# Top-k attention with a low-rank mixer on one core: side work of the vector engine handed to the scalar and pool engines

## The chip, the core and the metric

The kernel runs on one NeuronCore of a Trainium2 chip. Five engines take part, each with its own in-order queue of instructions. TensorE (PE, with its weight loads shown apart as PEld) does the matmuls and transposes. VectorE (DVE) does the search for the largest scores. ScalarE (ACT) does exponentials and copies out of PSUM. GpSimd (POOL) does elementwise work in SBUF. SyncE (SP) issues most transfers. The metric is the device time of one execution in microseconds (us). A result is the median over runs.

## What is computed

The attention keeps, for every query, only the 32 largest of 576 scores. Its output, with the heads laid side by side, is the input `x` of a mixer: a rank-32 map over the sequence is added to it (`u`), and a two-layer MLP over the channels is added to that.

```python
# q, k, v: (8, 8, 576, 64) fp32; U (576, 32), V (32, 576), w_ch1 (512, 2048), w_ch2 (2048, 512): fp64
scores = scale * q @ k.T
kth = the 32nd largest of each row
scores = where(scores >= kth, scores, -1e9)
attn = exp(scores - max); attn = attn / (attn.sum() + 1e-9)
x = (attn @ v), heads side by side          # (8, 576, 512)
u = x + (x.T @ U @ V).T
out = u + relu(u @ w_ch1) @ w_ch2
```

q, k and v are fp32. U, V and the two weight matrices arrive as 64-bit floats, and the kernel turns them into 32-bit floats by integer arithmetic on their words.

## The kernel before

**Pairs, tiles and steps.** The 64 heads are taken as 32 pairs `g`, four pairs to a batch. The 576 rows of a pair are five tiles `t`: tiles 0 to 3 have 128 rows and hold two score chunks of 128 x 576 (one for each head); tile 4 (`t == NT`) has the 64 last rows of both heads stacked into one chunk. One tile is one step `n`, so a pair has five steps and the run 160.

**One step.** `scores` does the matmuls, and ACT copies the scores to SBUF (lines 288 to 290; line 280 for tile 4). `front` then runs the search on DVE, for every chunk: MAX8 (line 315), then three times MATCH_REPLACE8 and MAX8 (lines 327 and 331). The 32nd value is the threshold. Chunk 0 is weighed early: ACT takes the exponential (line 295), and after the search one DVE operation zeroes what is under the threshold and sums the row (the mask, line 335). Chunk 1 goes the other way: after the search POOL adds -3e38 to scores under the threshold in two operations (lines 333 and 334), and ACT takes the exponential and the sum afterwards. Tile 4 has only chunk 0, so it is masked on DVE. `turns` transposes the weights on PE (line 363, and line 368 for the tails), with ACT copying them out; `values` multiplies by v (lines 383, 393 and 396).

**The mixer.** When a pair's five tiles are done, `mixed` transposes its output on PE (line 417), one DVE operation multiplies it by the reciprocals of the row sums into `x` (line 419), and some slots later PE multiplies by U (line 430) and V (line 442), giving `uT`. When a batch's four pairs are there, `mlp` starts: matmuls with w_ch1 (line 467), relu on ACT (line 479), matmuls with w_ch2 (line 486), one DVE operation that adds `uT` and writes `oT` (line 499), and `turned_back`, which transposes `oT` on PE (line 511) and stores it. `turned_back` is put off by a few matmuls (lines 480 and 493).

**The order.** PE and ACT run in exactly the order in which the program is written. DVE and POOL are ordered by a scheduler that goes by readiness in its own model of time, with `high_priority` blocks (lines 379, 418 and 498) put first when ready. The MLP of a batch is a generator; `fill` takes a measured share of it in eight slots of every step of the next batch, so that PE alternates between attention and MLP. The first 21 steps (`n <= ALONE`, batch 0) have no MLP to fill in. The MLP of batch 7 comes after the last step.

**The parameters.** 36 pieces of 64-bit parameters (four small ones for U and V, 32 of 128 x 512 for the weights) go through three buffers `raw`. One call of `next_params` joins the piece before (`f64_join`), splits the piece that has landed (`f64_parts`) and issues the next transfer on SP. Splitting is an Abs and an Identity on ACT (lines 152 and 154) and a maximum on POOL (line 153). Joining is a shift-and-mask on DVE (line 160), an and-or of the exponent's top bits from the high word on DVE (line 168) and an integer add on POOL of the low part (line 172), which is the last reader of `raw`. On DVE the join is ordered behind the last mask. One piece is taken in each step of batch 0, two in each step from step 21 until all are done.

Of the kernel before, what the change touches and what calls it, by code (L numbers as in the profile page):

```python
# [8 lines left out]
F32 = mybir.dt.float32  # L9
# [12 lines left out]
def kernel(  # L22
# [82 lines left out]
    half_bit = const.tile([P, 1], F32, name="half_bit")  # L105
    nc.vector.memset(half_bit, 1.0 / 64)
# [30 lines left out]
    def f64_parts(raw, out):  # L137


        n, w = raw.shape[0], raw.shape[-1] // 2  # L140
# [13 lines left out]
        nc.scalar.activation(low, low8, AF.Identity, bias=half_bit[0:n], scale=1.0 / 32)  # L154
        return hi, bits, low

    def f64_join(hi, bits, low, outs):


        ins = nc.vector.tensor_scalar(  # L160
            bits, bits, 3, 0x3FFFFFFF, ALU.logical_shift_left, ALU.bitwise_and
        )
        if last_mask:
# [4 lines left out]
        nc.vector.scalar_tensor_tensor(  # L168
            out=bits, in0=hi, scalar=0xC0000000, in1=bits, op0=ALU.bitwise_and, op1=ALU.bitwise_or
        )  # L170
# [47 lines left out]
    def load(g):  # L218
# [3 lines left out]
        for name, src in (("q", q), ("k", k)):  # L222
            queue = nc.scalar if g == 0 and name == "k" else nc.sync
            t = loads.tile([P, NT, 2, D], F32, tag=f"ld_{name}", name=f"ld_{name}")
            for i in range(2):
                queue.dma_start(
                    t[:, :, i, :],
                    src[b, h0 + i, 0:MAIN, :].rearrange("(p t) d -> p t d", t=NT),
                )
            queue.dma_start(  # L230
# [12 lines left out]
    def prep(g):  # L243
# [4 lines left out]
        for i, t in enumerate(tiles):  # L248
# [3 lines left out]
            nc.scalar.copy(qkT[:, i, 0:MAIN], tp.rearrange("p t n -> p (t n)"))  # L252
# [8 lines left out]
    def scores(g, t):  # L261
# [26 lines left out]
        nc.scalar.copy(main[:, :, 0:HALF], scs[0][:, :, 0:HALF])  # L288
# [8 lines left out]
    def front(g, t):  # L297
# [10 lines left out]
        probs[g, t] = E2  # L308
        curs, ms = list(chunks), [None] * n
# [13 lines left out]
        weigh(chunks[0], Es[0], nmax[:, 0:1])  # L323
        for i in range(1, TOPK // 8):
# [4 lines left out]
            for c in order:  # L329
                ms[c] = small.tile([P, 8], F32, tag="m8", name="m8", bufs=8)  # L330
                nc.vector.max(ms[c], curs[c])  # L331
        if n == 2:
            nc.gpsimd.tensor_scalar(Es[1], chunks[1], ms[1][:, 7:8], NEG, ALU.is_lt, ALU.mult)  # L333
            nc.gpsimd.tensor_tensor(chunks[1], chunks[1], Es[1], ALU.add)  # L334
        ins = nc.vector.scalar_tensor_tensor(  # L335
            out=Es[0],
            in0=chunks[0],
            scalar=ms[0][:, 7:8],
            in1=Es[0],
            op0=ALU.is_ge,  # L340
            op1=ALU.mult,
            accum_out=sums[0],
        )
# [4 lines left out]
        if n == 2:  # L348
            weigh(chunks[1], Es[1], nmax[:, 1:2], sums[1])
# [58 lines left out]
    def mixed(g, wait):  # L408
# [9 lines left out]
        with tc.high_priority():  # L418
            nc.vector.tensor_tensor(
# [37 lines left out]
    def mlp(b):  # L457
# [3 lines left out]
        for chunks, (lo, hi) in zip(PARTS, SPAN):  # L461
            w = hi - lo
            hTs = []
            for f in range(NF):
# [15 lines left out]
                if f == 1 and late:  # L480
                    late.pop()()
# [171 lines left out]
```

## Time and profile before

| | us |
|---|---|
| three runs | 1920.41, 1916.99, 1920.29 |
| median | 1920.29 |
| the profiled execution | 1917.73 |
| its span, first to last instruction | 1915.9 |

| engine | busy us | share of the span | instructions |
|---|---|---|---|
| PE | 1772.1 | 92% | 10528 |
| PEld | 1335.0 | 70% | 10528 |
| DVE | 1654.0 | 86% | 3433 |
| ACT | 953.4 | 50% | 2345 |
| POOL | 571.8 | 30% | 346 |

Busy time is the union of an engine's instructions. Idle time costs something only on the engine that sets the pace of a stage, and here this is not the same engine in all stages. The order of the masks on DVE gives a clock for the steps: the mask of step 0 starts at 22.38 us, that of step 20 at 247.65, of step 28 at 358.87, of step 40 at 485.40 and that of the last step, 159, at 1760.27.

### The profile page before, as it was taken

To read this page: it belongs to the slowest core of one execution; us is meant where nothing else is said; L and a number is where in the kernel's file an instruction comes from. 1 tells how busy PE (TensorE), PEld (TensorE's weight loads), DVE (VectorE), ACT (ScalarE), POOL (GpSimd) and SP (SyncE) were. 2 spreads that over 40 slices of the span, in tenths; PEclk is the share of its full clock that TensorE was granted. 3 is DMA by queue.
4 is the path that set the end of the run, shared out by engine and by line. 5 is a ranking of instruction groups with operands and counts; after the bars stand their busy time and mean duration, and the time that the engine had idled before them with its cause. 6 is when DMAs were issued, how large, how long until landed. Compare 5 with 4: busy or idle time off the path is not lost.

```text
span 1915.9 us, 29112 instructions
## 1 busy us (share of the span) xinstructions
PE 1772.1 (92%) x10528; PEld 1335.0 (70%) x10528; DVE 1654.0 (86%) x3433; ACT 953.4 (50%) x2345; POOL 571.8 (30%) x346
## 2 busy tenths in 40 slices
PE   5666688999899999999999999999999999999999
PEld 3444465687667877778677877778677877778777
DVE  7999998999999989999899999999899998997000
ACT  4555555554554545555555546555555545554111
POOL 3545556422332222222232222222232222232000
PEclk7767698999999999999999999999999999999999
DMA  2222222201001010100001010101001010000000
GB/s 72 72 60 59 68 74 79 58 17 28 23 20 30 24 30 15 27 18 23 25 20 30 23 31 15 27 15 26 25 20 31 22 31 15 15 8 7 6 14 11
DMA packets 127296, 58.21 MB, mean 30 GB/s; under 512 B 89905, under 2 KB 124977, under 8 KB 127153
## 3 DMA queue, kind: packets, MB, share of 16 engines
q1 hardware_dynamic: 125952, 56.06, 11.0%
q8 instruction: 83, 1.36, 0.3%
q14 instruction: 61, 0.49, 0.1%
q10 hardware_dynamic: 1200, 0.30, 0.1%
HBM read 46.89 MB, written 9.44 MB: 29 GB/s over the span
## 4 chain that ended last, share of the span: by engine, by line
PE 63%; DVE 26%; ACT 4%; issue 3%; POOL 3%; DMA 1%; DVEq 0%; SPq 0%; POOLq 0%; ACTq 0%
PE mm L467 21%; PE mm L486 18%; DVE rr L327 11%; DVE m L331 10%; PE sc L270 6%; PE O L396 5%; PE tp L363 4%; DVE first L315 2%; DVE E L335 2%; PE O L383 1%; PE up L442 1%; ACT E L295 1%; POOL E L333 1%; PE O L393 1%; PE tp L251 1%
## 5 line engine op out<-in xcount | busy, mean ns | idle before, releaser
L331 DVE MAX8 m<-rr 128x8 f32<-128x576 f32 x864 | 614.9, 747 | 4.0
L333 POOL TENSOR_SCALAR E<-Ssb,m 128x576 f32<-128x576 f32 x128 | 285.6, 2231 | 1089.2 <-DVE m L331 546.3
L467 PE MATMUL mm<-uT,w 128*128 128x256 f32 (+1 forms) x2048 | 559.7, 411 | 2.7 <-ACT hT L479 2.7
L486 PE MATMUL mm<-hT,w 128*128 128x256 f32 (+1 forms) x2048 | 560.4, 411 | 0.0
L467 PEld LDWEIGHTS mm<-uT,w 128*128 128x128 f32 x2048 | 364.0, 191 | 110.2 <-issue 30.5
L486 PEld LDWEIGHTS mm<-hT,w 128*128 128x128 f32 x2048 | 364.2, 191 | 100.2 <-issue 22.9
L327 DVE MATCH_REPLACE8 rr<-m,rr 128x576 f32<-128x576 f32 x576 | 427.8, 743 | 0.0
L315 DVE MAX8 first<-Ssb 128x8 f32<-128x576 f32 x288 | 215.6, 752 | 58.6 <-ACT Ssb L290 58.5
L364 ACT COPY PT<-tp 128x512 f32<-128x512 f32 x288 | 168.5, 585 | 187.1 <-PE tp L363 185.2
L363 PE MATMUL tp<-ident,E 128*128 128x128 f32 x1152 | 185.4, 286 | 81.3 <-ACT E L295 54.3
L363 PEld LDWEIGHTS tp<-ident,E 128*128 128x128 f32 x1152 | 144.7, 146 | 145.5 <-ACT E L295 69.1
L295 ACT ACTIVATE E<-Ssb,nmax 128x576 f32<-128x576 f32 x288 | 223.3, 776 | 11.2 <-POOL Ssb L334 5.9
L270 PE MATMUL sc<-qkT 64*128 64x288 f32 (+1 forms) x1280 | 213.9, 457 | 0.4 <-ACT qkT L252 0.4
L327 DVE MATCH_REPLACE8 rr<-first,Ssb 128x576 f32<-128x576 f32 x288 | 212.3, 742 | 0.0
L334 POOL TENSOR_TENSOR Ssb<-Ssb,E 128x576 f32<-128x576 f32 x128 | 188.0, 1469 | 10.6
L405 ACT COPY XT<-O 128x128 f32<-128x128 f32 x128 | 34.2, 267 | 248.9 <-PE O L396 248.9
L479 ACT ACTIVATE hT<-mm 128x320 f32<-128x320 f32 (+1 forms) x256 | 104.3, 408 | 106.7 <-PE mm L467 105.2
L499 DVE TENSOR_TENSOR oT<-uT,mm 128x320 f32<-128x320 f32 (+1 forms) x64 | 28.4, 444 | 146.4 <-PE mm L486 146.4
L396 PE MATMUL O<-PT,va 128*64 128x128 f32 x2048 | 154.2, 298 | 0.0
L270 PEld LDWEIGHTS sc<-qkT 64*128 64x128 f32 (+1 forms) x1280 | 111.2, 189 | 53.9 <-issue 27.3
L335 DVE SCALAR_TENSOR_TENSOR E<-Ssb,m,E 128x576 f32<-128x576 f32 x160 | 130.5, 815 | 18.5 <-ACT E L295 9.9
L396 PEld LDWEIGHTS O<-PT,va 128*64 128x64 f32 x2048 | 120.7, 147 | 17.1 <-issue 3.6
(68 smaller groups left out, 1378.1 us busy)
## 6 DMA issues: line engine op xcount, KB each, us to landing
raw<-in_moe_w_ch_dram SPq DMA_DIRECT2D x32, 512.0 KB, 3.8
ld_q<-in_q_dram SPq DMA_DIRECT2D x64, 128.0 KB, 2.8
va<-in_v_dram SPq DMA_DIRECT2D x64, 128.0 KB, 2.4
out_dram<-ob SPq DMA_DIRECT2D x64, 128.0 KB, 1.9
ld_k<-in_k_dram SPq DMA_DIRECT2D x62, 128.0 KB, 2.8
ld_ends<-in_q_dram SPq DMA_DIRECT2D x32, 32.0 KB, 2.2
vd<-in_v_dram SPq DMA_DIRECT2D x64, 16.0 KB, 2.0
vt<-in_v_dram SPq DMA_DIRECT2D x32, 32.0 KB, 2.3
```

Of the source, the lines that this page charges most:

```text
L270: nc.tensor.matmul(sc[slice(0, n) if t < NT else half(h), h, 0:HALF], lhsT=qkT[half(h), 0, cols(t)], rhs=qkT[half(h), 1, i * HALF : (i + 1 ...
L295: nc.scalar.activation(E, chunk, AF.Exp, bias=nmax, scale=SCALE, accum_out=total)
L315: ins = nc.vector.max(ms[c], curs[c])
L327: nc.vector.match_replace(nxt, ms[c], curs[c], NEG)
L331: nc.vector.max(ms[c], curs[c])
L333: nc.gpsimd.tensor_scalar(Es[1], chunks[1], ms[1][:, 7:8], NEG, ALU.is_lt, ALU.mult)
L334: nc.gpsimd.tensor_tensor(chunks[1], chunks[1], Es[1], ALU.add)
L335: ins = nc.vector.scalar_tensor_tensor(out=Es[0], in0=chunks[0], scalar=ms[0][:, 7:8], in1=Es[0], op0=ALU.is_ge, op1=ALU.mult, accum_out=s ...
L363: nc.tensor.transpose(tp[:, j, :], E2[:, a : a + P], ident)
L396: nc.tensor.matmul(O[half(h)], lhsT=va[:, h, j, :], rhs=PT[:, NT * h + j], start=False, stop=(j == NT - 1),)
L467: nc.tensor.matmul(ph[:, 0:w], lhsT=w1[:, cc, f * P : (f + 1) * P], rhs=uT[:, cc, lo:hi], start=(cc == 0), stop=(cc == NC - 1),)
L486: nc.tensor.matmul(po[:, 0:w], lhsT=w2[:, f, c * P : (c + 1) * P], rhs=hTs[f][:, 0:w], start=(f == 0), stop=(f == NF - 1),)
```

## The change

Six edits are made.

1. **Parameters.** The and-or on DVE (line 168) goes away. ACT gets a third operation for each piece, a Sign of the high word, written over the high word; the constants of the Identity change; the shift on DVE has one operation in place of two; POOL gets a second integer add (`bits + hi`) ahead of the one with the low part.
2. **x.** The DVE multiplication of `mixed` goes away. In batch 0 ACT does it as eight scaled copies of 128 x 64. In the other batches ACT copies PSUM to `x` and POOL multiplies in place. The number of slots before U's matmuls goes from 4 to 5 outside batch 0.
3. **u.** The DVE addition after w_ch2 becomes an ACT copy and a POOL addition, but for the last batch; `turned_back` is put off from the 4th matmul of the group to the 10th, and from the 2nd group to the 4th at the start of the next half.
4. **Tail masks.** From batch 1 on, tile 4 is masked by POOL like chunk 1 and weighed after it; the weighing of tile 4 is moved ahead of its transposes.
5. **First loads.** For the first pair, head 0 of q and k is loaded on SP and head 1 on ACT's queue, in place of q on SP and k on ACT's.
6. **First copies.** The first k transposes and the first half of the first scores are copied by DVE in place of ACT.

```diff
 def f64_parts(raw, out):
-        nc.scalar.activation(low, low8, AF.Identity, bias=half_bit[0:n], scale=1.0 / 32)
+        nc.scalar.activation(low, low8, AF.Identity, bias=step[0:n], scale=(1 + 2.0**-10) / 32)
+        nc.scalar.activation(hi.bitcast(F32), hi.bitcast(F32), AF.Sign, bias=nudge[0:n])
 def f64_join(hi, bits, low, outs):
-        ins = nc.vector.tensor_scalar(
-            bits, bits, 3, 0x3FFFFFFF, ALU.logical_shift_left, ALU.bitwise_and
-        )
+        ins = nc.vector.tensor_single_scalar(bits, bits, 3, ALU.logical_shift_left)
...
-        nc.vector.scalar_tensor_tensor(
-            out=bits, in0=hi, scalar=0xC0000000, in1=bits, op0=ALU.bitwise_and, op1=ALU.bitwise_or
-        )
+        nc.gpsimd.tensor_tensor(bits, bits, hi, ALU.add)
 def load(g):
-            queue = nc.scalar if g == 0 and name == "k" else nc.sync
...
+                queue = nc.scalar if g == 0 and i else nc.sync
 def prep(g):
-            nc.scalar.copy(qkT[:, i, 0:MAIN], tp.rearrange("p t n -> p (t n)"))
+            copy = nc.vector.tensor_copy if g == 0 and i else nc.scalar.copy
+            copy(qkT[:, i, 0:MAIN], tp.rearrange("p t n -> p (t n)"))
 def scores(g, t):
-        nc.scalar.copy(main[:, :, 0:HALF], scs[0][:, :, 0:HALF])
+        copy = nc.vector.tensor_copy if g + t == 0 else nc.scalar.copy
+        copy(main[:, :, 0:HALF], scs[0][:, :, 0:HALF])
 def front(g, t):
+        pooled = 1 if n == 2 else 0 if g >= NPAIR else None
...
-        weigh(chunks[0], Es[0], nmax[:, 0:1])
+        if pooled != 0:
+            weigh(chunks[0], Es[0], nmax[:, 0:1])
...
-        if n == 2:
-            nc.gpsimd.tensor_scalar(Es[1], chunks[1], ms[1][:, 7:8], NEG, ALU.is_lt, ALU.mult)
-            nc.gpsimd.tensor_tensor(chunks[1], chunks[1], Es[1], ALU.add)
-        ins = nc.vector.scalar_tensor_tensor(...)
+        if pooled is not None:
+            chunk, E = chunks[pooled], Es[pooled]
+            nc.gpsimd.tensor_scalar(E, chunk, ms[pooled][:, 7:8], NEG, ALU.is_lt, ALU.mult)
+            nc.gpsimd.tensor_tensor(chunk, chunk, E, ALU.add)
+        if pooled != 0:
+            ins = nc.vector.scalar_tensor_tensor(...)
...
-        if n == 2:
-            weigh(chunks[1], Es[1], nmax[:, 1:2], sums[1])
+        if pooled is not None:
+            weigh(chunks[pooled], Es[pooled], nmax[:, pooled : pooled + 1], sums[pooled])
 def mixed(g, wait):
-        with tc.high_priority():
-            nc.vector.tensor_tensor(X, tp, den, ALU.mult)
+        if g < NPAIR:
+            for t in range(NT):
+                for h in range(2):
+                    i = 2 * t + h
+                    nc.scalar.mul(X[:, t, half(h)], tp[:, t, half(h)], den[:, i : i + 1])
+        else:
+            nc.scalar.copy(X[:, 0:NT, :], tp)
+            nc.gpsimd.tensor_tensor(X4, X4, den, ALU.mult)
 def mlp(b):
-                if f == 1 and late:
+                if f == 3 and late:
...
-                    if f == 3 and late:
+                    if f == 9 and late:
...
-                with tc.high_priority():
+                if b == B - 1:
                     nc.vector.tensor_tensor(oT[:, 0:w], uT[:, c, lo:hi], po[:, 0:w], ALU.add)
+                else:
+                    nc.scalar.copy(oT[:, 0:w], po[:, 0:w])
+                    nc.gpsimd.tensor_tensor(oT[:, 0:w], oT[:, 0:w], uT[:, c, lo:hi], ALU.add)
 main loop, after batch 0
-            mixing.append(mixed((n - 2) // CH, 4))
+            mixing.append(mixed((n - 2) // CH, 5))
...
+        if n <= STEPS and t == 0:
+            next(fronts.pop(n - 1))
+            fill()
         if n <= STEPS:
             turning = turns(*divmod(n - 1, CH))
         next(turning, None)
         fill()
-        if n <= STEPS:
+        if n <= STEPS and t:
             next(fronts.pop(n - 1))
-        fill()
+            fill()
+        if n > STEPS:
+            fill()
```

## The prediction, made before the change was run

> **What bounds the kernel now.** I read the page's slices first: busy tenths and granted clock in 40 slices of 48 us.
>
> ```profile
> PE   5666688999899999999999999999999999999999
> DVE  7999998999999989999899999999899998997000
> PEclk7767698999999999999999999999999999999999
> ```
>
> In the first five slices DVE is full and PE is at six tenths of a reduced clock; later both are full; at the end PE works alone. Next, busy time by stage, cut at the masks that mark the steps (columns: stretch, its length, busy us and instructions of PE, PEld, DVE, ACT, POOL, clock, DMA).
>
> ```profile
> core 0: us, PE busy (x) PEld busy (x) DVE busy (x) ACT busy (x) POOL busy (x), PEclk, DMA share, GB/s
> 11.70:232.47 220.77, 138.03 (x733) 92.01 (x733) 210.94 (x444) 117.05 (x272) 113.23 (x73) 0.69 0.23 62
> 247.65:358.87 111.22, 94.33 (x503) 64.83 (x502) 101.32 (x200) 64.16 (x145) 70.33 (x45) 0.94 0.29 83
> 380.70:431.47 50.77, 50.77 (x332) 41.53 (x331) 49.95 (x105) 30.12 (x77) 14.98 (x9) 1.00 0.09 23
> 955.47:1171.34 215.87, 212.21 (x1317) 161.68 (x1316) 202.16 (x420) 113.85 (x285) 57.93 (x32) 1.00 0.09 24
> ```
>
> Three stages. **I** (to step 20, 247.65): DVE has work all the time. **II** (steps 20 to 28, to 358.87): two parameter pieces a step; eight steps take 13.9 us each, neither DVE nor PE is full. **III**: PE is the bound; a batch takes 215.87 us, of which PE idles 3.66. Then the waits: DVE's up to 240 us, PE's in one batch.
>
> ```profile
> DVE first L315 <- ACT Ssb L290: 10.9, 1, 10.9
> DVE x L419 <- PE tp L417: 6.3, 3, 2.5
> ```
>
> ```profile
> PE tp L511 <- DVE oT L499: 1.8, 1, 1.8
> PE tp L363 <- DVE x L419: 1.6, 1, 1.6
> ```
>
> After its start DVE waits in stage I for nothing but `x`. In stage III PE's idle time is 1.8 + 1.6 of waits for the very operations that the change moves. Last, the prices, from the groups with shapes kept apart:
>
> ```profile
> L168 DVE SCALAR_TENSOR_TENSOR w<-raw,w 128x512 uint32<-128x512 uint32 x32 | 24.5, 784 | 0.0
> L172 POOL TENSOR_TENSOR w<-w,raw 128x512 uint32<-128x512 uint32 x32 | 42.1, 1324 | 14.0 <-DVE w L168 14.0
> L333 POOL TENSOR_SCALAR E<-Ssb,m 128x576 f32<-128x576 f32 x128 | 285.6, 2231 | 1089.2 <-DVE m L331 546.3 <-PE mm L467 198.8 <-PE tp L363 125.2
> L334 POOL TENSOR_TENSOR Ssb<-Ssb,E 128x576 f32<-128x576 f32 x128 | 188.0, 1469 | 10.6
> L419 DVE TENSOR_TENSOR x<-tp,den 128x512 f32<-128x512 f32 x32 | 21.6, 676 | 11.5 <-PE tp L417 11.5
> ```
>
> **Stage I, DVE-bound: -23.7 us.** Line 168 goes: 19 operations up to 248 us, 11.3 busy. `x` goes: 4 x 0.69 = 2.8. DVE's stalls ahead of `x`, 6.3 up to 240 us and 2.8 at 241, go with it, since what stands next on DVE (the other chunk's search) needs nothing of the mixer: 9.1. The single-operation shift I leave at its 0.42. What takes the work: POOL adds 20 x 1.32 = 26 to its 113 of 221 us, behind the same step's mask pair, so DVE doesn't see it; ACT adds 20 Signs (nearest row: the Abs of line 152, 0.67) and eight scaled copies per pair (nearest row: line 391, 0.31 each, so 2.5 in place of DVE's 0.69), which lengthen the mixer's chain by 1.8; the scores for DVE's next step were copied out before it starts, so that is covered by a search of some 10 us. Without that cover it would cost 4 x 1.8 = 7.2. First loads: DVE's first search starts at 11.73; q's second half was issued behind its first on SP (1.61 us for both), now beside it; k's head 0 stands behind two q transfers. A gain of at most those 0.8 plus one 0.59 copy, a loss of at most one 0.65 issue: -1.4 to +0.65, I take -0.5, as the scores' matmuls (1.6) stay in the way of the second copy. Sum: 11.3 + 2.8 + 9.1 + 0.5 = 23.7; bounds 15 and 25.
>
> **Stage II, a loop through POOL and a transfer: +4 us.** The chain of waits by time:
>
> ```profile
> 266.92 3.35 DMA raw<-in_moe_w_ch_dram
> 270.29 0.67 ACT w L152
> 271.04 0.95 POOL w L153
> 279.16 3.33 DMA raw<-in_moe_w_ch_dram
> ```
>
> Each turn is: transfer 3.35, Abs 0.67, maximum 1.49, the step's mask pair 2.22 + 1.45, a second maximum 1.5, the add that frees `raw` 1.27, next transfer: 11.95 without the hand-overs, measured 12.24 from one transfer to the next and 14.86 to the one after. ACT stands still while it waits for the transfer (15.3 us in all, up to 5.3 at once), and behind its Abs are queued the copies that PE's transposes wait for. The new add stands ahead of the freeing one: +1.3 a turn, with 14 pieces left to fetch in pairs that is 7 turns, +9.1. Sign stands behind the Identity and delays only the second piece, 0.67, under the first one's POOL work. Against it: 331 to 358 us the chain runs through DVE, with two pairs of line 168 (1.28 and 2.48) and a 4.8 us wait ahead of `oT`; I count 5 of these 8.6 as gained, since POOL is next: its sum per step becomes 3.67 + 2 x (1.49 + 1.32 + 1.32) = 11.9, and the 4.0 of transfer and Abs are covered only by the second piece's 2.6, so a turn can't be under 13.3. Step 24, the tail, gets a POOL mask pair that it didn't have, inside that. Eight turns of 13.3 to 15 are 106 to 120 against 111: I take +4, bounds -12 and +14.
>
> **Stage III, PE-bound: -10 us.** PE's work is unchanged, so only its idle time counts: from 358.87 to 1760.27 it is 30.2 us (11.4 to 694 us, by such stretches, the rest at 3.66 a batch). All can go at best. New waits: `x` now passes ACT and POOL. In a batch's period, line 417 ends at 1026.7, ACT is free of its exponential at 1027.96, copies 0.59, and POOL needs 1.3 (line 172's row): 1029.9 if POOL is free. POOL gets the step's mask pair at 1028.84. Behind its first operation `x` is ready at 1032.4, behind both at 1033.9. U's matmuls stood at 1030.30 and move by a slot, an eighth of a 10.8 us step, to 1031.65: a wait of 0, 0.75 or 2.2. I take 0.5 x 28 pairs = 14. `oT`: the transposes move by six matmuls of 0.27 or 0.22; the chain is an ACT copy (0.43, row of line 479) and 0.74 to 0.89 on POOL (between 0.45 for 128 and 1.32 for 512 columns), 1.3 together against ten matmuls' 2.7, so a stall only if POOL has just begun a mask operation: up to 0.8 in some of 56, 0.1 x 56 = 6. Old 30 less new 20: gain 10, bounds: gain 28, loss 15. The tail masks take 0.9 off DVE, which isn't the bound here, and put 3.7 + 0.8 on POOL and ACT; `turns` of tile 4 starts more than 8 us after that search (1759.84 and 1768.61 at the end), so nothing shows; without this slack it would be 4.5 - 0.9 = 3.6 a pair. `u` of batch 7 stays on DVE: 0.
>
> A rule speaks against moving adds to POOL. The Trainium skill, "GPSIMD Engine Reference", section 4.1 "Engine selection", sends elementwise adds to VectorE and puts GpSimd at about twice the time for two inputs. The rows above say 1324 against 784 ns, 1.7 times. By the page's factor the new add would be 1.57 and the seven turns 11.0 in place of 9.1.
>
> **Sum.** 23.7 - 4 + 10 = 29.7, from the profiled 1917.7: 1888. The median of the runs shown stands 2.6 above that execution, its fastest run 0.7 below; I add 1: **1889**.
>
> **Rivals.**
> *The whole idle time goes* (stage II relaxes, the new waits don't come): 23.7 + 12 + 28 = 63.7, 1855. For it: ACT's stalls begin with late POOL adds, and those sat behind line 168. Against: POOL's sum.
> *POOL becomes the wait* (the slower side): POOL takes `x` and `oT` in order behind the mask pair, which waits for DVE's last MAX8. Price: 28 x 2.2 = 62 for `x`, 56 x 0.5 = 28 for `oT`, 90 less the old 30 is a loss of 60; with stages I and II 1917.7 + 60 - 19.7 = 1958. It decides from 50 us of new waits on, 1.8 a pair. For it: no priority block now puts these two first. Against: POOL is at 27% in stage III and takes what is ready.
> *DVE's relief is hidden in stage I*: the chain of mask, exponential, transposes and scores takes over and 9 of 23.7 remain: 1903. Against: DVE never waits for scores after the first.
> *The Sign costs table loads.* The trace has one load of 1.28 us (line 252) for Exp, Abs, Identity, Relu and copies. If Sign were in another table, 36 pieces x 2 x 1.28 = 92 us more on ACT; stage II's 17 pieces would show 44: about 1932. The Trainium skill, "ScalarE: Activation LUTs", section "Table sets: the hidden batching unit", says that cheap functions appear in every set; it names relu, copy, identity and abs, and no run here shows Sign.
>
> **Chances.** Forecast 0.62, all idle gone 0.17, POOL's wait 0.13, hidden 0.05, table loads 0.03. The forecast's own range, from its bounds without all falling together: 1866 to 1911. The one for 8 in 10 reaches a little into the relaxed case and to where POOL's wait eats the gain: 1863 to 1914. A measurement here tells 0.2%, some 4 us, from no change. Faster by more: 0.62 + 0.17 + 0.05 less 0.02 of the forecast's edge, 0.82; within: 0.02 of it and 0.02 of POOL's case, 0.04; slower: 0.11 + 0.03 = 0.14.
>
> **What would show it.** Stage I: the mask of step 20 (232.47 for step 19 before) some 23 us earlier. Stage II: the time from step 20 to 28 near 115 us, POOL over 85% busy, Abs still waiting for transfers. Stage III: a batch near 214.5 us, PE waiting for POOL at lines of U and of `oT`'s transposes, not for DVE. A batch of 218 us or more, or stage II over 125, makes the forecast wrong on the slow side; stage II under 100 on the fast side.

## The result, and the profile after

| | before | after |
|---|---|---|
| median of four runs each, us | 1919.32 | 1984.39 |
| span of the profiled execution, us | 1915.9 | 1982.6 |
| after over before, with its 95% interval | | 1.0341 (1.0323 to 1.0359) |

The kernel became slower by 65 us. The forecast was 1889 with a range up to 1914, so both its size and its sign are wrong. The page's slices of the changed kernel (busy tenths and granted clock, 40 slices of 50 us):

```profile
PE   5666687899999999999999999999999999999999
DVE  7899977888989998889789998889789998887000
POOL 3566677634333333334334343334333343343000
PEclk7676798999999999999999999999999999999999
```

DVE, which stood at nine tenths nearly everywhere, now falls to seven or eight tenths again and again, and POOL has a third more work (780.0 us busy against 571.8). What DVE gained in free time has not become speed. The same clock of masks as in the prediction (line 344 now) tells where the time went:

| stretch | before us | after us | difference |
|---|---|---|---|
| I, to step 20 | 247.65 | 241.16 | -6.5 |
| II, steps 20 to 28 | 111.22 | 118.59 | +7.4 |
| steps 28 to 60 | 335.20 | 351.01 | +15.8 |
| steps 60 to 158 | 1059.1 | 1107.6 | +48.5 |
| the rest | 162.7 | 164.2 | +1.5 |
| sum | 1915.9 | 1982.6 | +66.7 |

Busy time by stretch after: stages I and II, steps 28 to 60, and one batch of stage III (columns as in the prediction: stretch, length, busy us of PE, PEld, DVE, ACT, POOL, clock, DMA).

```profile
0.00:241.16 241.16, 151.19 (x799) 99.24 (x799) 214.36 (x453) 142.49 (x342) 133.62 (x110) 0.71 0.25 67
241.16:359.75 118.59, 95.71 (x508) 64.89 (x507) 94.25 (x180) 74.58 (x164) 90.14 (x63) 0.93 0.26 77
359.75:710.76 351.01, 329.79 (x2043) 253.46 (x2041) 315.44 (x635) 186.95 (x470) 139.16 (x89) 0.97 0.09 22
936.12:1161.64 225.52, 215.27 (x1318) 163.66 (x1316) 198.33 (x402) 120.60 (x301) 83.13 (x53) 0.98 0.09 23
```

The last row answers to the batch of 215.87 us, of which PE worked 212.21. The batch is 9.65 longer, in two parts: PE idles 10.25 in place of 3.66 (6.6 more), and needs 3.06 more for the same matmuls, at a clock of 0.98 in place of 1.00. What PE waited for in that batch (us in total, times, longest):

```profile
PE pT L446 <- POOL x L435: 5.9, 4, 2.3
PE tp L530 <- POOL oT L518: 3.4, 1, 3.4
```

The two waits for DVE of 1.8 and 1.6 are gone, and two kinds of wait for POOL stand in their place. Over the whole execution:

```profile
PE pT L446 <- POOL x L435: 46.1, 26, 6.3
PE tp L530 <- POOL oT L518: 18.2, 6, 3.4
```

How one for `x` arises is seen by time (start, duration, engine, line; in brackets the idle time before it and what ended it):

```profile
944.64 0.66 PE L426 MATMUL tp<-ident,XT 128*128 128x128 f32 x4
...
946.48 0.57 ACT L433 COPY x<-tp 128x512 f32<-128x512 f32 x1
...
946.94 2.21 POOL L341 TENSOR_SCALAR E<-Ssb,m 128x576 f32<-128x576 f32 x1 [3.67 <-DVE m L338]
...
949.23 1.41 POOL L342 TENSOR_TENSOR Ssb<-Ssb,E 128x576 f32<-128x576 f32 x1
...
950.61 1.04 POOL L435 TENSOR_TENSOR x<-x,den 128x512 f32<-128x512 f32 x1
...
951.70 0.62 PE L446 MATMUL pT<-x,U 128*32 128x128 f32 x10 [0.99 <-POOL x L435]
```

POOL is at 37% in this batch (83.13 of 225.52) and stands idle for 3.67 us, but its queue is in order: next in it is the mask pair of the running step (the two operations of lines 341 and 342), which waits for DVE's last MAX8. ACT's copy of `x` lands 0.1 us after that pair has begun, and the product gets its turn 3.6 us later, behind both. For 26 of the 28 pairs of heads the product starts right behind a mask pair; the mean over all 28 is 3.8 us after the copy. Further down the same queue an `oT` meets the same pair:

```profile
956.90 0.37 ACT L517 COPY oT<-mm 128x256 f32<-128x256 f32 x1
...
957.70 2.21 POOL L341 TENSOR_SCALAR E<-Ssb,m 128x576 f32<-128x576 f32 x1 [6.06 <-DVE m L338]
...
959.99 1.41 POOL L342 TENSOR_TENSOR Ssb<-Ssb,E 128x576 f32<-128x576 f32 x1
...
961.35 1.25 POOL L518 TENSOR_TENSOR oT<-oT,uT 128x256 f32<-128x256 f32 x1
...
962.65 0.44 PE L530 MATMUL tp<-ident,oT 128*128 128x128 f32 x2 [3.37 <-POOL oT L518]
```

Here the copy was done at 957.27, while POOL stood idle from 951.64 to 957.70, 0.43 us of it with the input ready; the addition still went behind the pair, and PE waited 3.37 us.

Stage II holds another wait of the same kind. POOL's and DVE's queues in one step of it:

```profile
267.37 2.22 POOL L341 TENSOR_SCALAR E<-Ssb,m 128x576 f32<-128x576 f32 x1 [3.66 <-DVE m L338]
269.67 1.47 POOL L342 TENSOR_TENSOR Ssb<-Ssb,E 128x576 f32<-128x576 f32 x1
271.11 1.50 POOL L157 TENSOR_SCALAR w<-w 128x512 f32<-128x512 f32 x1
```

```profile
272.64 1.51 DVE L167 TENSOR_SCALAR w<-w 128x512 uint32<-128x512 uint32 x1 [2.77 <-POOL w L157]
```

POOL idles 3.66 us before the pair with the piece's maximum (line 157) behind it, and then DVE waits 2.77 us for that maximum, since the shift (line 167) comes next on DVE. Before the change the same two stood the other way round on POOL:

```profile
271.04 1.49 POOL L153 TENSOR_SCALAR w<-w 128x512 f32<-128x512 f32 x1 [2.89 <-ACT w L152]
272.51 2.22 POOL L333 TENSOR_SCALAR E<-Ssb,m 128x576 f32<-128x576 f32 x1
```

The edit touched neither of these lines. POOL's order comes from a scheduler that goes by readiness in its own model of time. That the lighter DVE made the mask pair ready earlier in that model is my reading; the new order is what the trace shows. The run `only_p` below, the kernel before with the new rounding alone, has it too, so it comes with that edit:

```profile
289.01 2.30 POOL L333 TENSOR_SCALAR E<-Ssb,m 128x576 f32<-128x576 f32 x1 [3.67 <-DVE m L331]
291.40 1.40 POOL L334 TENSOR_TENSOR Ssb<-Ssb,E 128x576 f32<-128x576 f32 x1
292.77 1.49 POOL L156 TENSOR_SCALAR w<-w 128x512 f32<-128x512 f32 x1
```

DVE's waits of this sort in the changed kernel, in steps 20 to 28:

```profile
DVE w L167 <- POOL w L157: 21.0, 7, 6.1
```

Up to 240 us, where DVE waited for scores only at its start, it now does so again and again:

```profile
DVE first L321 <- ACT Ssb L295: 13.4, 6, 3.4
```

So the readings to test were: `x` behind the mask pair costs most of stage III; `oT` adds to it; the maximum behind the pair costs stage II; and in stage I ACT's new work (Sign, scaled copies) has become the pace.

### The profile page after: what moved, and what is told of

It reads as the page before. It is cut to its first block, busy times and chain, and to the rows that moved or that the text cites. A ratio compares the mean times of both kernels' runs of the same rounds, so it can differ in the third digit from the quotient of the medians.

```text
span 1982.6 us, 29317 instructions
## 1 busy us (share of the span) xinstructions
PE 1792.7 (90%) x10528; PEld 1346.7 (68%) x10528; DVE 1609.9 (81%) x3256; ACT 1024.6 (52%) x2523; POOL 780.0 (39%) x522
## 4 chain that ended last, share of the span: by engine, by line
PE 48%; DVE 24%; POOL 7%; ACT 4%; issue 3%; POOLq 0%; ACTq 0%; DVEq 0%
PE mm L483 17%; PE mm L502 14%; DVE rr L334 11%; DVE m L338 8%; PE O L405 4%; PE sc L274 4%; POOL E L341 3%; PE tp L372 3%; DVE first L321 2%; POOL Ssb L342 2%; DVE den L389 1%; PE up L458 1%; POOL x L435 1%; DVE E L344 1%; PE O L402 1%
## 5 line engine op out<-in xcount | busy, mean ns | idle before, releaser
L341 POOL TENSOR_SCALAR E<-Ssb,m 128x576 f32<-128x576 f32 x156 | 346.3, 2220 | 871.9 <-DVE m L338 658.5
L483 PE MATMUL mm<-uT,w 128*128 128x256 f32 (+1 forms) x2048 | 570.3, 419 | 1.3 <-ACT hT L495 1.3
L483 PEld LDWEIGHTS mm<-uT,w 128*128 128x128 f32 x2048 | 372.7, 194 | 113.3 <-issue 33.7
L342 POOL TENSOR_TENSOR Ssb<-Ssb,E 128x576 f32<-128x576 f32 x156 | 219.9, 1410 | 12.9
L344 DVE SCALAR_TENSOR_TENSOR E<-Ssb,m,E 128x576 f32<-128x576 f32 x132 | 108.9, 825 | 52.1 <-ACT E L300 46.9
L414 ACT COPY XT<-O 128x128 f32<-128x128 f32 x128 | 34.2, 267 | 214.5 <-PE O L405 214.5
L515 DVE TENSOR_TENSOR oT<-uT,mm 128x320 f32<-128x320 f32 (+1 forms) x8 | 3.6, 454 | 141.3 <-PE mm L502 141.3
```

The source lines that it names most:

```text
L341: nc.gpsimd.tensor_scalar(E, chunk, ms[pooled][:, 7:8], NEG, ALU.is_lt, ALU.mult)
L342: nc.gpsimd.tensor_tensor(chunk, chunk, E, ALU.add)
L483: nc.tensor.matmul(ph[:, 0:w], lhsT=w1[:, cc, f * P : (f + 1) * P], rhs=uT[:, cc, lo:hi], start=(cc == 0), stop=(cc == NC - 1),)
```

## The experiments

Fourteen runs of twelve kernels, with the stretches read from their own masks ("batch" is steps 80 to 100; in the changed kernel, and in those that keep its waits, other batches differ from it by up to 2 us). The kernel before, measured beside them, took 1920.58 us beside the first four, 1921.42 beside `x_first` to `mix1`, 1917.43 (nine runs) beside `max_first` to `mix1_not` and `mix1_r`, and 1918.56 (eleven runs) beside the last two. `mix1_r` and `mix1_not_r` are the kernels `mix1` and `mix1_not` again, in five and four runs; `whole_ordered` has eight, the others one each. Single runs of the kernel before spread over 5 us (1916.47 to 1921.42), so single runs that differ by less are not told apart by their times.

| kernel | time us | to step 20 | II | 28 to 60 | batch |
|---|---|---|---|---|---|
| before | 1919.32 | 247.65 | 111.2 | 335.2 | 215.87 |
| after | 1984.39 | 241.2 | 118.6 | 351.0 | 225.5 |
| no_x | 1925.13 | 247.4 | 118.5 | 340.9 | 214.4 |
| no_u | 1969.47 | 240.1 | 119.9 | 351.7 | 222.0 |
| no_p | 1972.06 | 235.9 | 111.5 | 349.8 | 225.6 |
| no_t | 2000.67 | 242.8 | 113.8 | 354.7 | 228.7 |
| x_first | 1933.16 | 240.8 | 118.7 | 332.0 | 218.8 |
| wait8 | 1926.63 | 239.8 | 118.9 | 335.8 | 216.4 |
| only_p | 1922.28 | 247.2 | 112.9 | 338.9 | 215.85 |
| mix1 | 1906.80 | 236.2 | 114.5 | 337.4 | 214.4 |
| max_first | 1966.93 | 241.4 | 104.6 | 345.9 | 225.4 |
| p_no_sign | 1914.34 | 239.8 | 112.7 | 338.4 | 215.87 |
| mix1_not | 1901.09 | 236.0 | 112.0 | 335.2 | 214.5 |
| mix1_not_r | 1899.88 | 236.0 | 109.6 | 337.0 | 214.5 |
| whole_ordered | 1914.48 | 242.4 | 103.7 | 337.1 | 216.4 |

### One part undone at a time

**`x` back on DVE** (the change otherwise whole):

```diff
-        if g < NPAIR:
...
-        else:
-            nc.scalar.copy(X[:, 0:NT, :], tp)
-            nc.gpsimd.tensor_tensor(X4, X4, den, ALU.mult)
+        with tc.high_priority():
+            nc.vector.tensor_tensor(X, tp, den, ALU.mult)
...
-            mixing.append(mixed((n - 2) // CH, 5))
+            mixing.append(mixed((n - 2) // CH, 4))
```

> The change without its edit of x: the product is back on DVE ahead of other work, and U's matmuls wait 4 slots. Theory POOL-order (PE loses time because x and oT stand behind the step's mask pair on POOL): the wait of U's matmuls for POOL, 5.9 us a batch, and most of the 3.1 us that the lower clock costs go, the old 1.6 us of x's wait come back; a batch 225.5 to about 219, the run about 1984 - 40 = 1944. Theory DVE-late (DVE's new stalls ahead of its masks, 46.9 us, and the later search make everything behind it late): x is only where it shows; a batch stays over 223, the run over 1972.

It took 1925.13, 59 us less than the change whole, and a batch fell from 225.5 to 214.4, under that of before. Stage I rose back to 247.4, and stage II stayed at 118.5: with `x` on DVE stage III loses nothing, and stage II as much as before. The gain is more than either reading had expected, and more than the price of the waits for `x`: PE's waits for `oT` fell too, from 18.2 us to 5.5, though nothing was done for them. Why they fell was not followed.

**`u` back on DVE:**

```diff
-                if b == B - 1:
+                with tc.high_priority():
                     nc.vector.tensor_tensor(oT[:, 0:w], uT[:, c, lo:hi], po[:, 0:w], ALU.add)
-                else:
-                    nc.scalar.copy(oT[:, 0:w], po[:, 0:w])
-                    nc.gpsimd.tensor_tensor(oT[:, 0:w], oT[:, 0:w], uT[:, c, lo:hi], ALU.add)
```

The two delays of `turned_back` went back to 1 and 3 with it.

> The change without its edit of u: the addition after w_ch2 is back on DVE, and the transposes of oT come after 4 matmuls. POOL-order: 3.4 us a batch of PE's wait for oT and a third of the clock loss go, 1.8 come back: a batch about 222.8, the run about 1967. DVE-late: DVE gets 3.5 us a batch more to do, so the run is not faster than 1980.

1969.47, 15 us less; a batch 222.0. The waits for `x` stayed (47.5 us in 26), so the additions of `u` are not what `x` queues behind; they have a smaller price of their own.

**The old rounding of parameters:**

```diff
-        nc.scalar.activation(low, low8, AF.Identity, bias=step[0:n], scale=(1 + 2.0**-10) / 32)
-        nc.scalar.activation(hi.bitcast(F32), hi.bitcast(F32), AF.Sign, bias=nudge[0:n])
+        nc.scalar.activation(low, low8, AF.Identity, bias=half_bit[0:n], scale=1.0 / 32)
...
-        ins = nc.vector.tensor_single_scalar(bits, bits, 3, ALU.logical_shift_left)
+        ins = nc.vector.tensor_scalar(
+            bits, bits, 3, 0x3FFFFFFF, ALU.logical_shift_left, ALU.bitwise_and
+        )
...
-        nc.gpsimd.tensor_tensor(bits, bits, hi, ALU.add)
+        nc.vector.scalar_tensor_tensor(
+            out=bits, in0=hi, scalar=0xC0000000, in1=bits, op0=ALU.bitwise_and, op1=ALU.bitwise_or
+        )
```

> The change with the old rounding of the parameters (two DVE operations, one POOL add, no Sign). If the eight DVE waits for POOL's maximum (24.6 us, steps 21 to 29) are what holds stage II, step 20 to 28 goes from 118.6 to 105 or less; if the loop through the transfer holds it, to 111 as before. Stage I gets line 168 back, up to 11 us later at step 20 if DVE sets the pace there, under 4 if the chain through PE and ACT does. A batch in stage III stays at 225.5 by both theories. The run 1968 to 1990.

1972.06, 12 us less: step 20 came at 235.9 (5.3 earlier), stage II took 111.5 (7.1 less), a batch stayed at 225.6. In the changed kernel the new rounding, the part that takes most off DVE, thus cost time in both stages that it works in. For stage I the expectation had allowed only a later step 20 or the same. Stage II at 111.5 is what it had named for the loop through the transfer; `max_first` below speaks for the order instead.

**The tail masks back on DVE** (with the weighing of tile 4 where it was):

```diff
-        pooled = 1 if n == 2 else 0 if g >= NPAIR else None
...
-        if pooled is not None:
-            chunk, E = chunks[pooled], Es[pooled]
-            nc.gpsimd.tensor_scalar(E, chunk, ms[pooled][:, 7:8], NEG, ALU.is_lt, ALU.mult)
-            nc.gpsimd.tensor_tensor(chunk, chunk, E, ALU.add)
-        if pooled != 0:
-            ins = nc.vector.scalar_tensor_tensor(...)
+        if n == 2:
+            nc.gpsimd.tensor_scalar(Es[1], chunks[1], ms[1][:, 7:8], NEG, ALU.is_lt, ALU.mult)
+            nc.gpsimd.tensor_tensor(chunks[1], chunks[1], Es[1], ALU.add)
+        ins = nc.vector.scalar_tensor_tensor(...)
```

> The change with the tail masks on DVE as before and the old place of the weighing. POOL-order: nothing but 3.6 us a pair of POOL's work goes, none of it in front of x or oT: a batch within 2 us of 225.5, the run 1975 to 1990. DVE-late: DVE's stalls ahead of its masks (up to 7.2 us, in the step after a tail) go, and a batch falls under 220, the run under 1950.

2000.67: slower by 16 us, though POOL had less to do. PE's waits for `x` grew from 46.1 to 63.1 us, again 26 of them, the longest 7.2. Neither reading had expected that, but it is not POOL's load that sets these waits. `x` stands behind the mask pair as before, and further behind: its product starts 4.5 us after ACT's copy on average, against 3.8 in the change. That is 0.65 us more for each of 28, and the waits grew by 17.0. That the mask pair comes later because DVE does the tail's mask was not taken apart further.

### Order or work: the same work in another order

If the price is the order on POOL and not the work given to it, it must go with all the work left in place.

**`x` ahead of the mask pair.** The pair is written one slot later, and its first operation is ordered behind the product of `x`:

```diff
+            low = nc.gpsimd.tensor_scalar(E, chunk, ms[pooled][:, 7:8], NEG, ALU.is_lt, ALU.mult)
+            if x_muls:
+                tc.add_manual_dep(low.ins, x_muls.pop(), mybir.DependencyInfo(
+                    mybir.DependencyClass.NoSync, mybir.DependencyReason.DATA
+                ), reason="order")
...
-            nc.gpsimd.tensor_tensor(
+            mul = nc.gpsimd.tensor_tensor(
...
+            x_muls.append(mul.ins.name)
```

> The change with one thing other: POOL's product for x is ordered ahead of the first mask operation of the step that is searched at that time, where it stood behind both. No engine has more or less to do. POOL-order: PE's wait for x, 5.9 us a batch, shrinks to under 1, and with it most of the clock loss of 3.1; a batch 217 to 219, the run about 1984 - 45 = 1940 (1930 to 1950). If the way over two engines is itself too long (the copy on ACT 0.57, the product 1.04, and what stands before the copy on ACT), the wait stays over 4 us a batch and the run over 1970.

1933.16, 51 us less. PE no longer waits for POOL's `x`, whose product now starts 0.08 us after the copy; `oT`, which nothing was done for, still costs a wait in each batch (PE's waits in one batch of this kernel):

```profile
PE tp L536 <- POOL oT L524: 4.4, 1, 4.4
PE tp L377 <- ACT E L300: 0.9, 3, 0.5
```

The later slot alone does not do it: `max_first` below also writes the pair one slot later, 25 of its 28 products still start right behind a pair, and a batch takes 225.4.

**U's matmuls eight slots later in place of five.** POOL's order stays; only its reader comes later:

```diff
-            mixing.append(mixed((n - 2) // CH, 5))
+            mixing.append(mixed((n - 2) // CH, 8))
```

> The change with U's matmuls put off by 8 slots in place of 5, POOL's order as it was. POOL-order: the longest waits in stage III are 2.3 us, three slots are some 4 us, so the wait for x goes to near 0 and a batch to 217 to 219, the run 1930 to 1950. If instead x's loss were the load on POOL and ACT (the work itself), nothing changes: 1980.

1926.63, 58 us less by one number, and the product still starts 3.7 us after the copy. One batch of it:

```profile
910.96:1127.37 216.41, 212.60 (x1318) 161.48 (x1317) 199.31 (x401) 119.13 (x301) 82.51 (x53) 1.00 0.09 23
```

PE idles 3.8 and works 212.60 at a clock of 1.00: both parts of the loss went, the idle time and the slower matmuls. POOL's work is much the same (82.5 us against 83.1 in the change). PE's waits for `oT` fell along with those for `x`, to 7.9 us in 6, the longest 1.3; why was not followed.

**The maximum ahead of the mask pair** in stage II:

```diff
-        nc.gpsimd.tensor_scalar(bits.bitcast(F32), bits.bitcast(F32), TINY, None, ALU.max)
+        top = nc.gpsimd.tensor_scalar(bits.bitcast(F32), bits.bitcast(F32), TINY, None, ALU.max)
+        maxima.append(top.ins.name)
...
+            cut = nc.gpsimd.tensor_scalar(E, chunk, ms[pooled][:, 7:8], NEG, ALU.is_lt, ALU.mult)
+            if g >= NPAIR and maxima:
+                tc.add_manual_dep(cut.ins, maxima[-1], mybir.DependencyInfo(
+                    mybir.DependencyClass.NoSync, mybir.DependencyReason.DATA
+                ), reason="order")
+                maxima.clear()
```

The pair is written one slot later here too; `x_first`, which has that without this order, stayed at 118.7 in stage II.

> The change with POOL's order altered while parameters are still being rounded: in each step from 21 on, the maximum of the first piece is ordered ahead of the step's first mask operation, as it stood in the kernel before. Theory order: DVE's waits for POOL's maximum (24.6 us in 8 waits) go, and steps 20 to 28 fall from 118.6 to 100 to 108. Theory load (the prediction's: POOL's added work and the loop through the transfer set the turn): the waits shift to the transfer or to the adds, and the eight steps stay within 4 us of 118.6. The run is read by these steps alone, since POOL's order in stage III may move too: 1960 to 1990.

Stage II fell from 118.6 to 104.6, with the same POOL work in it (91.37 us against 90.14). DVE's waits for the maximum in that stretch fell by half:

```profile
DVE w L168 <- POOL w L157: 9.8, 6, 4.4
```

A batch of stage III stayed at 225.4, so the two prices are separate. The 118.6 was an order too; with it mended, a step takes 13.1 us, a little less than the 13.3 a turn that the prediction held to be its floor. The order is not equally dear everywhere: `only_p` has it without the tail masks on POOL, and stage II takes 112.9 there, with 13.8 us of waits for the maximum; the change with the tail masks back on DVE (`no_t`) takes 113.8.

**The whole change with both orders mended** (the maximum first, and eight slots):

> All of the change's work on the engines that it chose, with two of its orders mended: POOL's maximum ahead of the mask operation in the steps that round parameters, and U's matmuls put off by 8 slots. If order and slots are the whole cause, the parts add: step 20 at 240, steps 20 to 28 in 105, a batch 216.4, the run 1926.6 - 14 = 1912, a ratio of 0.995 to 0.998 to the kernel before. If the moved work has a price of its own on POOL and ACT beyond the Sign, the run stays over 1920.

1914.48 (eight runs, 1911.26 to 1919.07), 0.9981 of before (0.9971 to 0.9992). All six edits are in, POOL does 780.3 us of work as in the change (780.0), and 70 us are gone. So what the changed kernel lost was lost by order, and the price of the moved work, less the relief that it brings DVE, is near nothing; the Sign's price, which comes next, is still in it. The gain over before is some 4 us by the medians, 2.3 by the spans of the profiled executions (1913.6 and 1915.9): stages I and II give 12.7 (242.4 and 103.7), and 1.9 to step 60, 3.6 to step 158 and 4.9 behind it are lost again.

### Stage I: what ate the relief

**The new rounding alone**, in the kernel before (the diff of `no_p` the other way round):

> The kernel before with the new rounding of the parameters and nothing else. From the run without x's edit (step 20 at 247.4 with the new rounding against 247.65, steps 20 to 28 in 118.5 against 111.2) the new rounding gains nothing in stage I, where PE's and ACT's chain sets the pace, and loses 7 us in stage II: the run 1920 to 1930, step 20 at 247 +- 2, steps 20 to 28 in 115 to 120. By the prediction's reckoning it would gain 11 in stage I and lose 4 in stage II: 1911.

Step 20 at 247.2: the and-or on DVE is gone, DVE's busy time in the stretch is 215.8 us in place of 223.3, and the gain is 0.5. Its waits for scores up to 240 us:

```profile
DVE first L315 <- ACT Ssb L290: 17.8, 6, 10.6
```

10.9 in one wait became 17.8 in six. The suspect was the Sign: 0.65 us more a step on ACT (from a Sign's start to the next operation's), ahead of the copies that PE's next scores and DVE's next search wait for.

**The same without the Sign** (the sign of the parameters is left out, so the mixer's numbers differ; POOL's addition still runs, with the high word as it is):

```diff
-        nc.scalar.activation(hi.bitcast(F32), hi.bitcast(F32), AF.Sign, bias=nudge[0:n])
```

> The kernel before with the new rounding, leaving out the Sign (the parameters' sign and range are then not mended, so the numbers of the mixer differ). If Sign, 0.65 us on ACT ahead of the copies that PE's transposes wait for, holds stage I, step 20 falls from 247.2 to 234 to 238, the 11.3 us of line 168 at last gained. If POOL's added add or DVE's own order holds it, step 20 stays over 244.

Step 20 at 239.8, 7.3 earlier, with the same work on DVE (215.3 us), and just short of the 234 to 238 expected. Up to there POOL's order is the same in both, and DVE's but for the place of `x`. The waits for scores up to 240 us:

```profile
DVE first L314 <- ACT Ssb L289: 10.6, 2, 10.3
```

Behind the start 0.3 us of waiting is left. The Signs up to step 20 hold ACT for 12.3 us in `only_p`; 7.3 of it stood on the path. From step 20 on the two kernels agree to 0.5 us (112.9 and 112.7, 338.9 and 338.4, 215.85 and 215.87): the Sign costs nothing there.

### What of the change is worth keeping

From these: the old rounding, `x` on ACT in batch 0 and on DVE after it with four slots, and the rest of the change.

```diff
         if g < NPAIR:
             for t in range(NT):
                 for h in range(2):
                     i = 2 * t + h
                     nc.scalar.mul(X[:, t, half(h)], tp[:, t, half(h)], den[:, i : i + 1])
         else:
-            nc.scalar.copy(X[:, 0:NT, :], tp)
...
+            with tc.high_priority():
+                nc.vector.tensor_tensor(X, tp, den, ALU.mult)
```

> The change with the old rounding, and with x on DVE from batch 1 on (batch 0's x stays on ACT). From the runs so far the parts add up: stage I as without the new rounding, step 20 at 236 (247.65 before); steps 20 to 28 in 111; a batch 214.4 as without x's edit (215.9 before). The run 1920 - 12 - 0 - 8 = 1900, and 1895 to 1908 if the stretch from step 28 to 60 keeps up to 6 of it. If the parts do not add, over 1915.

> The mixed version again, in rounds against the kernel before: 1906.8 in one look, against 1920 a ratio of 0.993; POOL-order expects it to hold, 0.991 to 0.995. If the one look was luck, the interval reaches 0.998.

1906.80 in one run, then 1905.38 in five (1904.64 to 1906.78): 0.9938 of before (0.9925 to 0.9952). A batch is 214.4; that the forecast had 214.5 is luck, since it had `x` on POOL.

**The same with the tail masks on DVE**, as in `no_t`:

> The mixed version (old rounding, x on ACT in batch 0 and on DVE after, u on ACT and POOL) with the tail masks on DVE again. By POOL-order the tail masks matter only through x's place behind the mask pair; with x on DVE a batch stays within 1 us of 214.4 and the run within 4 us of 1907. If the tail masks on POOL give DVE room that PE feels, a batch is 216 or more.

> The mixed version without tail masks on POOL again, in rounds: 1901.1 in one look, 4 us under the mixed version with them. Its trace puts 1.4 us of that in steps 20 to 28 and 2.2 in steps 28 to 60, none in stage III. A ratio of 0.990 to 0.993; if one look misled, it is the 0.9938 of the mixed version.

1901.09, then 1899.88 in four runs (1898.27 to 1901.16): 0.9900 of before (0.9883 to 0.9916). It beats both kernels, by 18.7 and 84.5 us. The tail masks on POOL cost some 5 us here, more than the 4 that the expectation had allowed, and nothing in a batch (214.5). Where exactly between step 20 and 60 isn't settled, since two executions of this kernel differ by 2.4 us in stage II (112.0 and 109.6) and by 1.8 the other way behind it (335.2 and 337.0).

## Why the prediction was wrong

**The failed step is stage III's price for `x`**: "a wait of 0, 0.75 or 2.2. I take 0.5 x 28 pairs = 14". Its working had the right parts: the copy on ACT (0.59 there, 0.57 measured), the product on POOL (1.3 there, 1.04), the mask pair that begins at the same moment, and 2.2 us if `x` comes behind both. It then took a value near nothing with "POOL is at 27% in stage III and takes what is ready" beside it. POOL took what was next in its queue, not what was ready: at 37% busy it stood idle 3.67 us waiting for DVE ahead of `x`, and 26 of 28 products started right behind a mask pair; PE waited for each of these, 46.1 us in all, 1.8 each. The row for "behind both" was the typical case. `x_first` shows that it is this order, and `wait8` that a later reader cures it as well.

**`oT`** was "0.1 x 56 = 6": it came to 18.2, and not as small waits at many places but as one wait in a batch, five times 3.4 us and once 1.3; where it is shown above, the addition fell behind the pair in the same way. Undoing `u` alone gave 15 us.

**A term was missing: the clock.** Both stalls were priced at their length. In the batch shown, PE's matmuls took 3.06 us more for the same work, a third of the batch's loss. From step 28 to 158, before and after:

```profile
358.87:1753.19 1394.32, 1364.59 (x8493) 1041.26 (x8492) 1316.10 (x2733) 736.39 (x1839) 379.70 (x211) 1.00 0.09 22
359.75:1818.40 1458.65, 1386.96 (x8494) 1056.29 (x8493) 1291.05 (x2602) 779.00 (x1943) 545.67 (x343) 0.98 0.08 21
```

Of the 64.3 us lost there, 42.0 are more idle time of PE (71.7 less 29.7) and 22.4 are slower matmuls.

**Stage II** was forecast at +4 and came to +7.4, inside its bounds, but the mechanism was another. The loop of transfer, Abs and freeing add was to grow by 1.3 a turn, with Abs still waiting for transfers; ACT's waits for transfers fell from 15.3 us to 4.2, and POOL was busy for 76% of the stage, not 85%. DVE waited for the maximum instead, because the order on POOL had turned. The 118.6 took both edits: 112.9 with the new rounding alone, 111.5 without it, 113.8 without the tail masks, whose place in stage II the forecast had set at nothing. With the order mended the stage took 104.6, 6.6 less than before; how much of that is the 5 us counted as gained from line 168 isn't shown.

**Stage I** was forecast at -23.7 and came to -6.5. The part of `x` and the start came in as worked out: 2.8 + 9.1 + 0.5 = 12.4 forecast, and with the old rounding (`no_p`) step 20 came 11.8 earlier. The first mask itself began at 21.58 in place of 22.38, 0.8 for the 0.5. Line 168's 11.3 didn't come in: 0.5 alone, and 5.3 lost on top of the rest. The claim that failed is "that is covered by a search of some 10 us". ACT's Sign (0.67 forecast for its duration, 0.756 measured) was counted and then set at nothing, because DVE waited for scores only at its start. That was true only as long as DVE was the slower chain: a wait of zero in a profile doesn't say how much room is left below it. The rival that saw the relief hidden in stage I (9 of 23.7 left) was right in this stage; I had weighed it alone, at 0.05.

**The rival that decided**, POOL becoming the wait, was given 0.13. Its mechanism, its place and its point of decision held: from 50 us of new waits on, and there were 64.3. Its loss of 60 in stage III compares with 64.3 measured from step 28 to 158, and that is in part luck: it had 90 us of waits for `x` and `oT` where 64.3 came, and no slower matmuls, which made up 22.4. Its 1958 fell short because it kept my stages I and II at a gain of 19.7; they lost 0.9.

**The other points.** The Sign needed no table of its own: the trace after has one load of 1.28 us, as before. A batch over 218 us was named as what would make the forecast wrong on the slow side, and 225.5 did. The tail masks were costed at nothing; in the change they were worth 16 us, with `x` closer behind its copy, and in `mix1` they cost 5.

## What to carry to other kernels

When a step is moved to an engine with time to spare, ask what stands ahead of it in that engine's order and what that waits for; the share of busy time says nothing about it, and a reader a few slots later (`wait8`, one number, 58 us) can be worth more than the whole move. An engine on which nothing waits today may have no room at all: price the chain that becomes the next bound before counting a relief as gained. And where a scheduler orders a queue by its own model, an edit on one engine can reorder work on another that the diff never names, so look at the order after, not only at the work.

## What the hardware showed that I had not expected

**A long stall of TensorE can be paid twice.** Granted clock in five stretches of 1 us behind the 3.37 us wait for `oT` (which ended at 962.65):

```profile
963.00:964.00 1.00, 1.00 (x5) 0.65 (x5) 1.00 (x3) 0.37 (x1) 0.00 (x0) 0.79 0.00 0
964.00:965.00 1.00, 1.00 (x4) 0.61 (x3) 1.00 (x3) 0.00 (x0) 0.00 (x0) 0.50 0.47 139
965.00:966.00 1.00, 1.00 (x3) 0.62 (x2) 1.00 (x3) 0.00 (x0) 0.00 (x0) 0.50 0.00 0
966.00:967.00 1.00, 1.00 (x5) 0.69 (x4) 0.97 (x3) 0.21 (x1) 0.00 (x0) 0.50 0.00 0
967.00:968.00 1.00, 1.00 (x6) 0.78 (x5) 1.00 (x3) 0.82 (x3) 0.00 (x0) 1.00 0.00 0
```

The clock (third number from the end) goes to half for some 3.4 us and then back. The same follows the wait of 2.28 us for `x` that ended at 1011.62 (0.69, 0.50, 0.50, 0.61, then 1.00: again some 3.4 us at half); behind the waits of 0.99 us at 951 and of 1.58 us at 1067 the clock stays at 1.00, and before's 1.8 and 1.6 cost none either. The Trainium skill, "TensorE: Matmul & The Clock Gate", section "HAM oscillation — how this bites in real kernels", warns of idle gaps over some 3.4 us, behind which the array starts at half rate. The 3.37 us stall agrees; the one of 2.28 us is shorter and was charged too, so here the measurement decides for a lower figure. Whether the light matmuls with U behind that stall, of 32 columns, count as idle time isn't shown by any run.

Length alone does not decide. Two waits of 1.97 us for `x` in the kernel after, which ended at 785.95 and 1236.84, were followed by these stretches:

```profile
787.00:788.00 1.00, 1.00 (x2) 0.67 (x3) 0.97 (x3) 0.21 (x1) 0.00 (x0) 0.50 0.00 0
1237.00:1238.00 1.00, 1.00 (x12) 0.69 (x5) 1.00 (x3) 0.27 (x1) 0.00 (x0) 1.00 0.00 0
```

And in the kernel before, two waits for `x` of 2.32 and 2.64 us, which ended at 442.3 and 490.4, cost no clock:

```profile
443.00:444.00 1.00, 1.00 (x6) 0.85 (x7) 1.00 (x3) 0.23 (x1) 0.92 (x2) 1.00 0.07 16
491.00:492.00 1.00, 1.00 (x7) 0.84 (x7) 1.00 (x4) 0.59 (x2) 0.00 (x0) 1.00 0.00 0
```

Where a wait falls seems to count. By the trace's clock records the stretches at half begin at 738.31, 786.10, 963.59, 1011.38 and 1188.87 us, and the steps between these times are 14, 52, 14 and 52 times 3.413 us: they lie on a grid. Cut at that grid, the waits for POOL from step 28 on that were charged have 1.96 us or more in one cell, those that went free 1.78 or less, and before's 2.32 and 2.64, cut at the grid of their own trace, at most 1.61. This border is no rule: in `no_x` a wait with 1.98 us in one cell went free.

**A small VectorE operation waits out a GpSimd one.** The constant that is added to a pair's row sums ahead of their reciprocal (128 x 9), after and before:

```profile
L389 DVE TENSOR_SCALAR den<-den 128x9 f32<-128x9 f32 x32 | 35.2, 1101 | 8.4 <-ACT E L300 8.4
```

```profile
L380 DVE TENSOR_SCALAR den<-den 128x9 f32<-128x9 f32 x32 | 5.2, 161 | 4.3 <-ACT E L295 4.3
```

It went from 161 to 1101 ns on average, the same operation on the same data. One of them started at 937.52, in the middle of POOL's line 342 (937.35 to 938.76), and ended at 938.79, with it. In every run with the tail masks on POOL its mean is 884 to 1101 ns, in every run without them 161 to 194. The Trainium skill, "Advanced Engine Details and Errata", section "Mode Summary", notes that VectorE's second port to SBUF is shared with GpSimd and that two-port operations of the one and GpSimd's block each other; these numbers agree with it, though no run shows that this operation uses both ports. The price, 30 us of DVE's time, fell in stages that DVE doesn't bound.

**Prices** that the prediction had to bound, from the groups after:

```profile
L435 POOL TENSOR_TENSOR x<-x,den 128x512 f32<-128x512 f32 x28 | 29.2, 1042 | 7.5 <-DVE m L338 5.8 <-ACT x L433 1.7
L518 POOL TENSOR_TENSOR oT<-oT,uT 128x320 f32<-128x320 f32 x28 | 24.2, 865 | 65.8 <-ACT oT L517 65.8
L518 POOL TENSOR_TENSOR oT<-oT,uT 128x256 f32<-128x256 f32 x28 | 23.0, 820 | 59.8 <-ACT oT L517 59.8
```

The product in place cost 1.04 us, under the 1.3 of the integer add of the same size, and the additions of `u` were inside their bounds. On average POOL's prices were right or too high; it was their place in the queue that the prediction had wrong.

**What stays open:** how much of the lower clock belongs to each kind of wait over the whole execution; the last 3.5 us of line 168's 11.3 that `p_no_sign` doesn't give back either (11.3 less the 7.8 by which its step 20 is earlier than before's); why the waits for `oT` shrink when those for `x` go in `no_x` and `wait8`; and how the scheduler's model came to the new order on POOL.
